# The last seven finished blocks of the first mixture are transposed by TensorE and copied by ScalarE instead of by a DMA transposition

## The chip, the cores and the metric

The kernel runs on one core of a Trainium2 chip. The metric is the device time of one execution, in microseconds (us). Engines are called by the names of the profile: PE is TensorE's matmul stream, PEld its weight loads, DVE is VectorE, ACT is ScalarE, POOL is GpSimd and SP is SyncE, which only issues DMAs here.

## What is computed

A banded attention over 3072 tokens, then two mixtures of experts in sequence. Cut to what matters here:

```python
x = attention(q, k, v, mem_k, mem_v)              # 3072 x 512
# first mixture: two experts per token
top2 = the two best of 8 noisy logits             # and their softmax weights
out[mask] += top2_w * (relu(x[mask] @ w1[e]) @ w2[e])
# second mixture: one expert per token, on the result of the first
logits = out @ w_gate2
expert_idx = argmax(logits); gate = softmax(logits)[expert_idx]
out2[mask] = gate * (relu(out[mask] @ w1b[e]) @ w2b[e])
```

The second mixture's routing needs its logits for every row that the first mixture produces, so the first mixture's last rows stand between the two.

## The kernel before

**Tiling.** Both mixtures work on blocks of 128 gathered rows. A group is two or three blocks of one expert. The first mixture has 17 groups (numbers 0 to 16, class `Moe1`); the last two, 15 and 16, are expert 7 with three blocks each, and group 16 also carries 32 remainder rows. The remainders of four experts are put together into one more block, which is finished under group number 15. For one group `mlp` does, per hidden slice f = 0 to 7, 12 matmuls into a PSUM tile `ph` (three buffers; L543), which ACT (L545) and DVE (L546) turn into the high and low fp16 halves of `hT`; then, per block, 24 matmuls of 512 columns into `py` (L554). The second mixture (`Moe2`) starts with three early groups whose rows are known before the first mixture is done, and goes on with late groups after a second routing.

**What a finished block does.** `Moe1.finish` scales `py` into `y` (ACT, L654; `y` has three buffers), scatters `y` to DRAM from POOL (L657), makes the high half of an fp16 pair `x16` (called `w` in the code; ACT, L671; two buffers) and starts a chain `rest`: DVE makes the low half (L675), a DMA on SP's queue transposes the 128 x 1024 pair into `xt` (L677), PE multiplies `xt` by the second router's weights into `lg` (`gating`, L240 and L241, eight small matmuls), DVE adds the two parts into `l` (L686) and POOL scatters `l` into the logits L in DRAM (L657).

**What sets the order.** Every engine runs its instructions in program order, and that order is written by hand: the main loop yields after each piece of a group, and a `Driver` keeps a modelled time, in which each chain sleeps for the number that it yields. The chain `rest` yields 1.2 before the low half and 8.5 after the DMA transposition. Two other chains stand in the stretch of interest: `first` (starts when groups 0 to 14 are finished) and `second` (when all are); each loads L (`lt`, L776), computes the chosen experts on DVE, counts on PE (L227 to L232), and builds a table with two `onehots` on DVE (L507 to L510) and 24 matmuls on PE (L813). From the first one's `etop` and the second one's `etab` SP reads which experts' weights to load (`stage`, L74); ACT and DVE convert these to fp16 pairs (L127, L128) between the other work. POOL gathers the second mixture's rows by the tables (`xp`, L1018), adds their halves (L1049, into an `x16` buffer), ACT and DVE make the pair `xg` (L1051, L1052), and SP's queue transposes it (L1061).

**Names for the seven blocks.** a1, a2, a3 are the blocks of group 15, b1, b2, b3 those of group 16, and r is the remainder block.

The chain that the change touches ends in these lines:

```python
t = parts("xt", 3)
nc.sync.dma_start_transpose(out=t.rearrange("p a k q -> p (a k) q"), in_=w)
yield 8.5
```

Of the kernel before, what the change touches and what calls it, by code (L numbers as in the profile page):

```python
# [6 lines left out]
F32 = mybir.dt.float32  # L7
F16 = mybir.dt.float16
I32 = mybir.dt.int32
U32 = mybir.dt.uint32  # L10
AF = mybir.ActivationFunctionType
# [171 lines left out]
def constants(tc, g, tmp):  # L183
    nc, c = tc.nc, g.c
# [7 lines left out]
    d = iota("diag", 128, F32, cm=-1, pool=tmp)  # L192
    g.ident = tmp.tile([128, 128], F32, name="ident")
    nc.vector.tensor_scalar(g.ident, d, 0.0, None, op0=OP.is_equal)
    g.ident16 = tmp.tile([128, 128], F16, name="ident16")
    nc.vector.tensor_scalar(g.ident16, d, 0.0, None, op0=OP.is_equal)
    g.tri = c.tile([128, 128], F16, name="tri")
    nc.vector.tensor_scalar(g.tri, d, 0.0, None, op0=OP.is_gt)
# [17 lines left out]
    for name, vals in (("prof", PROF), ("base", BASE[:8])):  # L216
        t = c.tile([128, E], F32, name=name)
# [19 lines left out]
def gating(nc, out, xT, w, n):  # L237

    for k in range(4):
        nc.tensor.matmul(out[:, 0:2 * n], xT[:, 0, k, :], w[:, :, k, :], start=(k == 0), stop=False)  # L240
        nc.tensor.matmul(out[:, n:2 * n], xT[:, 1, k, :], w[:, 0, k, :], start=False, stop=(k == 3))  # L241
# [321 lines left out]
class Moe1:  # L563
# [86 lines left out]
    def finish(self, p, gate, idx, group=None, lg=None):  # L650

        nc, g, tc = self.nc, self.g, self.tc
# [12 lines left out]
        def parts(name, n):  # L665
            if lg is None:
                return g.rr.tile([128, 2, 4, 128], F16, name=name, bufs=n)
            t = g.mo.tile([128, DM], F32, name="y", bufs=3).bitcast(F16)
            return t.rearrange("p (a k q) -> p a k q", a=2, k=4)
        w = parts("x16", 2).rearrange("p a k q -> p (a k q)")  # L670
        nc.scalar.activation(w[:, :DM], y, AF.Copy, scale=SX2)  # L671

        def rest(lg):
            yield 1.2
            nc.vector.scalar_tensor_tensor(w[:, DM:], y, SX2, w[:, :DM], op0=OP.mult, op1=OP.subtract)  # L675
            t = parts("xt", 3)
            nc.sync.dma_start_transpose(out=t.rearrange("p a k q -> p (a k) q"), in_=w)  # L677
            yield 8.5
            while not self.ready:
                yield 1.0  # L680
            if lg is None:
                lg = g.psr.tile([128, TB, 32], F32, name="lg")[:, 0]
            gating(nc, lg, t, g.wg2, E)
            l = g.mo.tile([128, E], F32, name="l", bufs=4)
            with nc.allow_low_precision("float32"):
                nc.vector.tensor_reduce(l, lg[:, 0:2 * E].rearrange("p (a e) -> p e a", a=2), axis=AX.X, op=OP.add)  # L686
            scatter(self.L, l)
            if group is not None:
                self.open.remove(group)
# [852 lines left out]
```

## Time and profile before

| | |
|---|---|
| median of 3 runs | 1035.58 us (1028.32 to 1047.32) |
| profiled execution, its own time | 1033.13 us |
| its span, first to last instruction | 1031.4 us |
| mean granted TensorE clock | 0.969 |
| PE busy | 951.9 us (92%) |
| DVE, ACT, POOL busy | 504.7, 386.3, 479.4 us |

The profile is of one execution. A timeline row gives start, length, engine, line, operation, and in brackets the idle time of that engine just before it with what ended it. A length of "x12" is that of twelve instructions from the first start to the last end. The granted clock is the share of full speed that TensorE was given: 1.00 is 2.4 GHz, 0.50 is 1.2 GHz.

### The profile page before, as it was taken

Reading aid. Unit: us, or ns where it says so; the run is one execution under the profiler, and the core shown is the slowest. Engines: PE = TensorE matmul, PEld = TensorE weight load, DVE = VectorE, ACT = ScalarE, POOL = GpSimd, SP = SyncE. Lnnn points to the kernel's source line nnn. Section 1 sums busy time; section 2 is a strip of 40 time slices with the busy share of each in tenths; the row PEclk is TensorE's granted clock in tenths of the full one; section 3 lists DMA queues with packets and bytes.
Section 4 is the critical chain, followed back from the end, with each engine's and each line's share of the span. In section 5 each row is a group of like instructions: output and inputs, shape, how many; then the busy total and the mean of one; then the engine's idle time right before and its main releaser. Section 6 shows DMA issues by size and latency. Waiting matters only on the chain.

```text
span 1031.4 us, 18755 instructions
## 1 busy us (share of the span) xinstructions
PE 951.9 (92%) x7259; PEld 566.5 (55%) x7259; DVE 504.7 (49%) x1032; ACT 386.3 (37%) x653; POOL 479.4 (46%) x484
## 2 busy tenths in 40 slices
PE   5897868999989999999999999985889999999998
PEld 4786745656545555455554555542457555555665
DVE  7689885642423443244332443473475436565511
ACT  2453444322323343333433343252423345454421
POOL 6755653334545454645546354335522635443421
PEclk9998969999999999999999999988899999999999
DMA  9999959745746686678766676489535879987720
GB/s 214 253 258 256 237 137 273 178 90 121 189 100 172 164 186 158 154 169 190 170 160 162 152 177 143 131 256 194 96 121 147 219 184 263 287 217 211 148 56 19
DMA packets 189218, 180.75 MB, mean 175 GB/s; under 512 B 152148, under 2 KB 153044, under 8 KB 188352
## 3 DMA queue, kind: packets, MB, share of 16 engines
q1 hardware_dynamic: 166736, 131.24, 54.2%
q0 software_dynamic: 21952, 48.07, 15.8%
q8 instruction: 60, 0.98, 0.4%
q14 instruction: 38, 0.31, 0.1%
q10 hardware_dynamic: 432, 0.15, 0.1%
HBM read 118.27 MB, written 39.53 MB: 153 GB/s over the span
## 4 chain that ended last, share of the span: by engine, by line
PE 41%; issue 16%; POOL 8%; DMA 4%; DVE 2%; ACT 0%; POOLq 0%; DVEq 0%; ACTq 0%
PE ph L543 19%; PE py L554 19%; POOL x L1049 2%; POOL xp L1018 2%; POOL out_dram L1068 2%; POOL gs L1018 2%; DMA stage<-in_v_dram 1%; PE py L736 1%; DMA xp<-Y,ter 1%; DMA xp<-Y,tbr 1%; DMA gs<-Pa,ter 1%; DMA out_dram<-y,teo 0%; DVE hT L546 0%; DMA xt<-x 0%; DVE w L128 0%
## 5 line engine op out<-in xcount | busy, mean ns | idle before, releaser
L543 PE MATMUL ph<-xT,w 128*128 128x384 f16 (+3 forms) x2688 | 426.5, 318 | 19.9 <-DVE hT L546 10.4
L554 PE MATMUL py<-w,hT 128*128 128x512 f16 x1800 | 394.2, 379 | 0.0
L543 PEld LDWEIGHTS <-w 128*128 128x128 f16 x2688 | 262.5, 99 | 166.8 <-issue 24.5
L554 PEld LDWEIGHTS <-hT 128*128 128x128 f16 x1800 | 175.7, 98 | 207.0
L546 DVE SCALAR_TENSOR_TENSOR hT<-ph,hT 128x384 f16<-128x384 f32 (+3 forms) x224 | 115.9, 521 | 218.0 <-ACT hT L545 216.9
L128 DVE SCALAR_TENSOR_TENSOR w<-stage,w 128x1024 f16<-128x1024 f32 x128 | 167.2, 1309 | 66.5 <-ACT w L127 66.3
L545 ACT ACTIVATE hT<-ph 128x384 f16<-128x384 f32 (+3 forms) x224 | 103.3, 463 | 212.6 <-PE ph L543 209.0
L127 ACT ACTIVATE w<-stage 128x1024 f16<-128x1024 f32 x128 | 133.6, 1049 | 19.1 <-DMA stage<-in_v_dram 14.3
L654 ACT ACTIVATE y<-py,gs 128x512 f32<-128x512 f32 x48 | 32.9, 686 | 176.4 <-PE py L554 170.3
L657 POOL DMA_INDIRECT L<-l,t3y x43 | 44.5, 1035 | 109.6 <-DVE l L686 106.2
L675 DVE SCALAR_TENSOR_TENSOR x<-y,x 128x512 f16<-128x512 f32 x50 | 34.4, 688 | 123.0 <-ACT x L671 122.9
L657 POOL DMA_INDIRECT Y<-y,t3y x43 | 44.8, 1041 | 91.5 <-ACT y L654 85.7
L1068 POOL DMA_INDIRECT out_dram<-y,tbo x20 | 20.8, 1039 | 110.8 <-ACT y L1067 89.0
L316 PE MATMUL s<-x 128*64 128x64 f32 x768 | 49.6, 287 | 16.3 <-DMA x<-in_xe_dram 11.6
L611 POOL DMA_INDIRECT Y<-ol,late x48 | 56.4, 1175 | 16.4 <-issue 16.4
L316 PEld LDWEIGHTS s<-x 128*64 128x64 f32 x768 | 46.3, 209 | 17.8 <-POOL x L303 8.3
L1067 ACT ACTIVATE y<-py,gs 128x512 f32<-128x512 f32 x27 | 18.6, 687 | 94.8 <-PE py L554 64.1
L370 POOL TENSOR_TENSOR x<-x,x 128x512 f16<-128x512 f32 x24 | 29.4, 1226 | 45.8 <-DVE x L369 25.1
L585 POOL DMA_INDIRECT xg<-X,t3x x43 | 42.0, 976 | 15.1 <-issue 14.6
L585 POOL DMA_INDIRECT gs<-G,t3g x41 | 38.7, 944 | 12.5 <-issue 12.5
L303 POOL COPY x<-x 24x780 f32<-24x780 f32 x48 | 41.0, 855 | 5.2 <-issue 2.5
L1049 POOL TENSOR_TENSOR x<-xp 128x512 f32<-128x512 f32 x27 | 35.9, 1355 | 15.1 <-DVE xg L1052 11.7
(276 smaller groups left out, 708.1 us busy)
## 6 DMA issues: line engine op xcount, KB each, us to landing
stage<-in_w_dram SPq DMA_DIRECT2D x64, 512.0 KB, 4.1
stage<-in_v_dram SPq DMA_DIRECT2D x64, 512.0 KB, 5.1
x<-in_xa_dram SPq DMA_DIRECT2D x24, 286.0 KB, 5.5
X<-x SPq DMA_DIRECT2D x24, 256.0 KB, 4.4
x<-in_xd_dram SPq DMA_DIRECT2D x24, 194.0 KB, 6.7
x<-in_xb_dram SPq DMA_DIRECT2D x24, 188.5 KB, 6.6
x<-in_xc_dram SPq DMA_DIRECT2D x24, 184.0 KB, 6.0
x<-in_xe_dram SPq DMA_DIRECT2D x24, 96.5 KB, 5.6
```

Source lines behind the costliest of these rows:

```text
L127: nc.scalar.activation(hi, src, AF.Copy, scale=SW)
L128: return lambda v=nc.vector: v.scalar_tensor_tensor(lo, src, SW, hi, op0=OP.mult, op1=OP.subtract)
L316: nc.tensor.matmul(s[o:o + 64, ch // 2, b], q[:, b, ch], k[:, b, 40 * ch:40 * ch + 64], start=True, stop=True)
L543: nc.tensor.matmul(p[:, :n], w1[:, a, k, f, :], xT[:, b, k, :n], start=(i == 0), stop=(i == 11))
L545: nc.scalar.activation(hT[:, 0, f, :n], p[:, :n], AF.Relu)
L546: nc.vector.scalar_tensor_tensor(hT[:, 1, f, :n], p[:, :n], 0.0, hT[:, 0, f, :n], op0=OP.max, op1=OP.subtract)
L554: nc.tensor.matmul(p[:m], hT[:, a, f, o:o + m], w2[:, c, f, :], start=(i == 0), stop=(i == 23))
L585: self.nc.gpsimd.indirect_dma_start(out=out, out_offset=None, in_=src, in_offset=IO(ap=idx, axis=0))
L611: st = nc.gpsimd.indirect_dma_start(out=self.Y, out_offset=IO(ap=idx[:, i:i + 1], axis=0), in_=z, in_offset=None, bounds_check=2 * N - 1, ...
L657: st = nc.gpsimd.indirect_dma_start(out=dst, out_offset=IO(ap=idx, axis=0), in_=src, in_offset=None, bounds_check=2 * N - 1, oob_is_err=False)
L1049: nc.gpsimd.tensor_tensor(s, x[:, :DM], x[:, DM:], op=OP.add)
L1068: st = nc.gpsimd.indirect_dma_start(out=self.out, out_offset=IO(ap=idx, axis=0), in_=y, in_offset=None, bounds_check=N - 1, oob_is_err=False)
```

## The change

For the blocks with a group number above 14 (a1 to b3 and r, seven in all), the DMA transposition is replaced by eight TensorE transposes of 128 x 128 into a `ph` tile of PSUM and one ACT copy of 128 x 1024 fp16 into `xt`. The chain's sleeps become 0.8 before and 1.0 after, instead of 8.5 after. The fp16 identity moves to the pool that lives through the whole kernel. Behind L677 all lines of the changed kernel are nine higher.

```diff
-    g.ident16 = tmp.tile([128, 128], F16, name="ident16")
+    g.ident16 = c.tile([128, 128], F16, name="ident16")
     nc.vector.tensor_scalar(g.ident16, d, 0.0, None, op0=OP.is_equal)
...
             t = parts("xt", 3)
-            nc.sync.dma_start_transpose(out=t.rearrange("p a k q -> p (a k) q"), in_=w)
-            yield 8.5
+            if group is not None and group > len(self.groups) - 3:
+
+                yield 0.8
+                o = g.pm.tile([128, 512], F32, name="ph", bufs=3).bitcast(F16).rearrange("p (i q) -> p i q", i=8)
+                for i in range(8):
+                    nc.tensor.transpose(o[:, i, :], w[:, 128 * i:128 * i + 128], g.ident16)
+                nc.scalar.activation(t.rearrange("p a k q -> p (a k) q"), o, AF.Copy)
+                yield 1.0
+            else:
+                nc.sync.dma_start_transpose(out=t.rearrange("p a k q -> p (a k) q"), in_=w)
+                yield 8.5
```

On PE, behind the first routing's count (L232) and the last block of group 15 (L554), this stood before: the 24 matmuls of a3, the hidden slice f0 of group 16, and then the gating of a1.

```order
7539 L232 MATMUL misc<-oh_8062,ones 128x8
7540 L554 LDWEIGHTS hT
7541 L554 MATMUL py<-w_2513,hT 128x512
...
7589 L554 MATMUL py<-w_2513,hT 128x512
7590 L543 LDWEIGHTS w_2512
7591 L543 MATMUL ph<-xT,w_2512 128x416
...
7614 L240 LDWEIGHTS xt
7615 L240 MATMUL lg<-wg_2518,xt 128x16
```

At the same place of the changed kernel (x_8051 is a1's pair, x_8097 a2's):

```order
7539 L232 MATMUL misc<-oh_8062,ones 128x8
7540 L682 LDWEIGHTS x_8051
7541 L682 MATMUL ph<-ident_117,x_8051 128x128
...
7556 L554 LDWEIGHTS hT
7557 L554 MATMUL py<-w_2513,hT 128x512
...
7620 L682 LDWEIGHTS x_8097
7621 L682 MATMUL ph<-ident_117,x_8097 128x128
...
7636 L543 LDWEIGHTS w_2512
7637 L543 MATMUL ph<-xT,w_2512 128x416
```

The transposes of a1 now stand ahead of a3's matmuls, the gating of a1 in the middle of them (not shown), and the transposes of a2 ahead of the whole of group 16. The transposes of a3 follow between f1 and f2.

On DVE, the low half of a2's pair (x_8097) stands in the changed kernel behind a weight conversion (L128) and the first routing's second one-hot pair, and behind it the next conversion and the low half of f0:

```order
868 L128 SCALAR_TENSOR_TENSOR w_2514<-stage,w_2514 128x1024
869 L507 TENSOR_TENSOR ol<-wide,lo_8176 128x1536
870 L509 TENSOR_TENSOR ov<-wide,col_8178 128x96
871 L510 TENSOR_TENSOR ov<-ov,tokb 128x96
872 L695 TENSOR_REDUCE l<-lg 128x8
873 L675 SCALAR_TENSOR_TENSOR x_8097<-y,x_8097 128x512
874 L128 SCALAR_TENSOR_TENSOR w_2514<-stage,w_2514 128x1024
875 L546 SCALAR_TENSOR_TENSOR hT<-ph,hT 128x416
876 L128 SCALAR_TENSOR_TENSOR w_2514<-stage,w_2514 128x1024
877 L695 TENSOR_REDUCE l<-lg 128x8
878 L675 SCALAR_TENSOR_TENSOR x_8255<-y,x_8255 128x512
```

That order is the one of before with one row put in: the sum of a1's logits (row 872) stood later.

On ACT, around the last block of group 16 and the remainder block, this stood before (`w_72` is a weight tile of the second mixture):

```order
417 L654 ACTIVATE y<-py,gs 128x512
418 L671 ACTIVATE x_8595<-y 128x512
419 L654 ACTIVATE y<-py,gs 128x512
420 L671 ACTIVATE x_8630<-y 128x512
421 L741 ACTIVATE x_8698<-py 64x512
422 L654 ACTIVATE y<-pr,gr 128x512
423 L671 ACTIVATE x_8706<-y 128x512
424 L127 ACTIVATE w_72<-stage 128x1024
425 L545 ACTIVATE hT<-ph 128x384 x2
```

And in the changed kernel:

```order
422 L683 ACTIVATE xt<-ph 128x1024
423 L654 ACTIVATE y<-py,gs 128x512
424 L671 ACTIVATE x_8679<-y 128x512
425 L683 ACTIVATE xt<-ph 128x1024
426 L750 ACTIVATE x_8756<-py 64x512
427 L654 ACTIVATE y<-pr,gr 128x512
428 L671 ACTIVATE x_8764<-y 128x512
429 L127 ACTIVATE w_72<-stage 128x1024
430 L683 ACTIVATE xt<-ph 128x1024
431 L545 ACTIVATE hT<-ph 128x384
432 L683 ACTIVATE xt<-ph 128x1024
```

The copies of b1 and b2 (the first two L683) stand around b3's `y`; the copy of b3 (the third) stands behind the remainder's three steps and a weight conversion, and the copy of r behind f0 of the second mixture's first group. On PE the gating of b3 follows b3's transposes at once (not shown).

## Rows read from the trace of the kernel before

**Rows 1.** Waits of PE, whole span: who waited for whom, total us, times, longest.
```profile
PE lg L240 <- DMA xt<-x: 15.9, 2, 11.9
```

**Rows 2.** Timeline of PE, 600 to 840 us.
```profile
660.15 5.34 PE L554 MATMUL py<-w,hT 128*128 128x512 f16 x24
...
667.64 4.38 PE L543 MATMUL ph<-xT,w 128*128 128x416 f16 x24
676.10 0.19 PE L240 MATMUL lg<-wg,xt 128*128 128x16 f16 x1 [4.07 <-DMA xt<-x]
...
676.34 4.32 PE L543 MATMUL ph<-xT,w 128*128 128x416 f16 x12
...
692.04 15.70 PE L554 MATMUL py<-w,hT 128*128 128x512 f16 x72
707.67 1.48 PE L736 MATMUL py<-w,rh 128*32 128x512 f16 x24
721.03 0.20 PE L240 MATMUL lg<-wg,xt 128*128 128x16 f16 x1 [11.88 <-DMA xt<-x]
...
746.54 7.93 PE L554 MATMUL py<-w,hT 128*128 128x512 f16 x36
...
763.31 5.40 PE L543 MATMUL ph<-xT,w 128*128 128x256 f16 x48
771.50 1.47 PE L543 MATMUL ph<-xT,w 128*128 128x256 f16 x12 [2.79 <-DVE hT L546]
...
778.07 5.34 PE L554 MATMUL py<-w,hT 128*128 128x512 f16 x24
...
791.33 10.64 PE L543 MATMUL ph<-xT,w 128*128 128x256 f16 x96
...
814.12 15.78 PE L543 MATMUL ph<-xT,w 128*128 128x384 f16 x96 [1.79 <-DMA xT<-xg]
```

**Rows 3.** Windows of PE: us, sum, busy (instructions), granted clock, DMA share, GB/s.
```profile
685.00:686.00 1.00, 1.00 (x7) 1.00 0.86 324
712.00:713.00 1.00, 0.00 (x0) 0.65 1.35 212
726.00:727.00 1.00, 1.00 (x11) 1.00 0.00 0
```

**Rows 4.** Timeline of PE in the attention: eight transposes, then the next matmul.
```profile
106.78 0.62 PE L383 MATMUL xp<-ident,x 128*128 128x128 f16 x8
107.24 0.18 PE L240 MATMUL lg<-wr,xt 128*128 128x32 f16 x1
```

**Rows 5.** Groups of ACT by form: busy us, mean ns, idle before and its releaser.
```profile
L384 ACT ACTIVATE xt<-xp 128x1024 f16<-128x1024 f16 x22 | 22.2, 1008 | 8.8 <-PE xp L383 8.8
```

**Rows 6.** Timeline of ACT, 640 to 815 us.
```profile
667.53 1.06 ACT L127 ACTIVATE w<-stage 128x1024 f16<-128x1024 f32 x1 [7.06 <-DMA stage<-in_v_dram]
...
725.64 0.59 ACT L741 ACTIVATE x<-py 64x512 f32<-64x512 f32 x1 [3.93 <-DMA xt<-x]
727.01 0.69 ACT L654 ACTIVATE y<-pr,gr 128x512 f32<-128x512 f32 x1 [0.78 <-DVE pr L742]
...
728.26 1.04 ACT L127 ACTIVATE w<-stage 128x1024 f16<-128x1024 f32 x1
```

**Rows 7.** Timeline of DVE, 640 to 815 us.
```profile
668.62 1.23 DVE L128 SCALAR_TENSOR_TENSOR w<-stage,w 128x1024 f16<-128x1024 f32 x1 [1.70 <-ACT w L127]
...
670.99 0.69 DVE L675 SCALAR_TENSOR_TENSOR x<-y,x 128x512 f16<-128x512 f32 x1
```

**Rows 8.** The tile xt, 640 to 780 us: the DMA transpositions from issue to landing.
```profile
DMA to landing us min/median/max: 3.1/4.3/19.2
```

**Rows 9.** Timeline of POOL at b1's scatter.
```profile
708.41 1.02 POOL L657 DMA_INDIRECT Y<-y,t3y  x1 [0.30 <-issue]
```

**Rows 10.** Issues of DMAs, 640 to 760 us: a scatter of y's size, us to landing.
```profile
out_dram<-y,teo POOLq DMA_INDIRECT x2, 7.1
```

**Rows 11.** Waits of PE, 810 to 1032 us.
```profile
PE ph L543 <- DVE hT L546: 3.5, 3, 1.9
```

## The prediction

> **What bounds the kernel now.** I read the waits of PE first, since PE is busy nine tenths of the span: what it waits for is what a change can give back. One wait for the operand of the second gating (`xt`, transposed by DMA) stands at the head, 15.9 us in two pieces [rows 1]. The timeline of PE places them [rows 2]: 4.07 us before 676.10, at a2, and 11.88 us before 721.03, at b1. The reader is to see that PE itself runs dry there; no other engine covers it. The tile view says why the second is long: a transposition landed 4.3 us after issue in the median and 19.2 us at worst [rows 8].
>
> The waits cost more than their length. The granted clock fell some 3 us into the second idle stretch (0.65 in 712 to 713) and came back at 685 and at 726 [rows 3], that is 8.9 and about 4.9 us after PE had work again. In between it is the 1.2 GHz level: 12 matmuls of 416 columns took 4.32 us [rows 2], where 24 took 4.38 at 2.4 GHz.
>
> So three stretches matter, by their ends in [rows 2]: A, from a3's matmuls (660.15) to the first `py` of group 16 (692.04), 31.9 us; B, from there to the first `py` of the second mixture (746.54), 54.5 us; C, the eight hidden slices of its next group (763.31 to 778.07), 14.8 us where the same 96 matmuls take 10.6 at 791.33. In C the releaser is DVE: 2.79 us for `hT`, because the second routing's table work stands in DVE's order between the slices.
>
> From 814 on PE waits 1.79 us for `xT` [rows 2] and 3.5 us for `hT` [rows 11], in 217 us. What is gained before 814 reaches the end.
>
> **The added work.** Eight transposes took 0.46 us from start to the next matmul at full clock [rows 4]; seven times that is 3.2 us of PE. One copy of 128 x 1024 took 1.008 us on ACT [rows 5]; seven are 7.1 us, on an engine with idle time but in an order that matters. Seven DMA issues leave SP's queue, so the later weight loads, the load of L and the transpositions of `xg` can only go earlier; I price that at nothing, since PE's waits after 814 are 5.3 us in all, and that is the most they could give. Moving the identity costs nothing: it is made once, at the start, as before.
>
> **Stretch A.** After the count at 660.15: transposes of a1 0.46, a3's 24 matmuls 5.2, gating 0.2, so PE is at a2's transposes at 666.0. They need a2's low half. On DVE it stands behind a weight conversion that waits for ACT's half of it, which in turn waited 7.06 us for its staged weights and began at 667.53 [rows 6]; DVE's half began at 668.62, and the low half of a2 at 670.99 with 0.69 us [rows 7]. None of this moves: the staged load follows the count, which is not later than before. With one small sum put ahead of it, the low half is ready at 671.8. Before, PE had f0 to f2 to do meanwhile (667.64 and ahead); now the transposes stand ahead of f0 and PE idles from 666.3 (four transposes need only the high half) to 671.8, 5.5 us instead of 4.07. Queued behind them is all of group 16, and the first routing's table, on which POOL's gathers wait.
>
> Then, at half clock: the other four transposes 0.4, f0 4.1 and gating 0.2, to 676.6. If the clock comes back as quickly as at 726, f1 takes 2.1 and PE waits for a3's low half (behind f0's `hT` on ACT and DVE, 0.5 and 0.6, and a conversion of 1.06 and 1.23) until about 679.9, then 0.4: 680.3. If as slowly as at 685, f1 ends at 680.8 and the transposes at 681.5. The rest, f2 to f7 (six of 2.1), gating 0.2 and 24 small table matmuls 0.7, is 13.6: `py` starts at 693.9 or 695.1. **A: 1.9 to 3.1 us longer, taken 2.5.**
>
> **Stretch B.** From the first `py`: two blocks 10.4, b1's transposes 0.5, half a block 2.6, gating 0.2 (its copy has 2.6 us of cover), half a block 2.6, b2's transposes 0.5, 24 remainder matmuls 1.4 (at 707.67 [rows 2]): 18.1. The copy for b2 stands on ACT behind b3's `y` and high half (about 1.25 together, the distance from 727.01 to 728.26 [rows 6]), so its gating waits about 0.7. Gating 0.2, the other 24 matmuls 1.4: 20.4.
>
> Here is the new wait. b3's transposes end at 20.9, but their copy stands on ACT behind the remainder's steps and a weight conversion. From the start of L741 to the end of that conversion took 3.66 us (725.64 to 728.26 and 1.04 [rows 6]); with the copy 1.0 and handovers 0.3, b3's gating starts at 25.4, a stall of 4.5. A further term: the remainder's `y` needs the buffer of b1's, whose scatter POOL started at 708.41 [rows 9]. POOL's gathers ahead of it follow the table, which is 3.4 to 4.6 later, so about 711; a scatter of that size took 7.1 to land [rows 10]. By that, up to 1.8 us more, at the other end nothing; I take 0.9, as POOL's issue after the table may be closer than before. That gives 26.3.
>
> Gating 0.2; f0 at half clock 3.9 (384 columns; full 1.97 from 15.78 for 96 [rows 2]); r's transposes 0.8; f1 2.0 or 3.9 by the two returns of the clock; gating 0.2; f2 to f7 11.8; 0.5 for the second count, which now stands ahead of `py`: 45.7 or 47.6. **B: 8.8 to 6.9 shorter, taken 7.9.** Not removed, then: of 11.88 plus half-clock work, a wait of about 5 with its own half-clock work stays.
>
> **Stretch C.** The second routing's count moves from the middle of the first group's `py` to ahead of it, so its chain on DVE runs under 15.7 us of `py`, not between the slices. Before, the count began at about 754.4 (746.54 and 7.93) and PE got on with the slices 17.1 us later, at 771.50; now `py` and the first slices, 1.3 each, cover that length. 14.8 becomes 10.6 and 0.5 that I leave for conversions: **C: 3.7 shorter.** If the count comes as late as before, nothing.
>
> **Sum.** +2.5 - 7.9 - 3.7 = -9.1. The profiled execution took 1033.13, so 1024.0. The median of the runs is 1035.58, 2.4 above it; runs lay from 1028.32 to 1047.32.
>
> **A rule against the change.** Rows: PE was granted full clock at 726 after 4.9 us of work, and in the attention, eight transposes among other matmuls took 0.46 us, 57 ns each [rows 3, 4]. The Trainium skill ("TensorE: Matmul & The Clock Gate", Part 4: PE-mode transpose) says that transposes do not count as busy for the clock and gives about 275 ns for one in a kernel. By that figure, an estimate from the page, 56 transposes one after another would be 15.4 us instead of 3.2. The rows at 106.78 do not agree, since they follow each other much closer.
>
> **The rivals.**
> - *Everything comes back* (0.10). A to C lose 4.07 and 11.88 in waits, 4.2 in C, and some 12 at half clock and in small waits behind, less 3.2 of transposes: about -29, 1004. For: the only releaser that PE names is the DMA. Against: DVE's 670.99 [rows 7] is later than the point at which PE now wants the pair.
> - *New waits take nearly all* (0.22). In B a weight conversion ahead of b3's copy waits for its staged load as one did for 7.06 us [rows 6], or the buffer of `y` comes 1.8 late, and the second count is not hidden (C gives nothing): -9.1 + 5 + 3.7 = -0.4, 1033. For: ACT and PE both work in order and ACT has waited so. Against: the load in question is issued long before.
> - *Slower: the clock stays down* (0.06). Transposes scattered behind each stall keep TensorE at 1.2 GHz through the three `py` of group 16 (15.7) and f2 to f7 of the next group (11.8); each costs its length again: -9.1 + 27.5 = +18, 1051. It decides against the change once more than 9.1 us of work that was at full clock runs at half. The page above would have it so. For: both returns took 5 us or more. Against: long matmul runs lie between the batches.
> - *The forecast* (0.62): 1024, its own range 1017 to 1031.
>
> **How the numbers follow.** The range leaves out the first rival and the slower one, 0.16, and a little of the tails; it takes in the forecast's bounds and the second rival with 2 or 3 us for the runs' own spread: 1012 to 1036. A measurement of this kernel can tell about 2% from no change, here 21 us. Faster by more needs the first rival or part of it: 0.10. Slower by more needs the clock rival at its full price and more: 0.03. Within 2%: 0.87.
>
> **What would show it.** In the changed profile PE should wait for DVE's low half ahead of f0 of group 16, about 5.5 us (A right), and for ACT's copy ahead of b3's gating, about 4.5 to 5.5 (B right), with 0.50 of the clock behind each; the wait for `xt` by DMA should be gone from these blocks. The eight slices of C should take 10.6 to 11.5 us, and everything from the first late group on should look as before, shifted. Wrong if a2's pair is ready by 667, if the gating of b3 finds its copy done, if the clock stays at 0.50 through `py`, or if a wait that is new arises after 814.

## The result, and the profile after

The changed kernel takes 1047.78 us in the median (1041.55 to 1051.8, 20 runs), the kernel before, run beside it, 1042.76 (1028.32 to 1047.32, 20 runs). The ratio is 1.0104, interval 1.0084 to 1.0124. Ratios are of executions not marked as slow: that leaves out some of the kernel before and none of the changed one here, so this ratio says 11 us where the two medians lie 5.0 apart, and the traces of before and before_again are of executions so marked. So the change costs 0.5% to 1%; forecast were 1024 and a gain of 9 us. The profiled execution of the changed kernel took 1046.33 us, with a span of 1044.6.

Lines behind L677 stand 9 further down now: L736 is L745, L741 is L750. L682 is the eight transposes of a block, L683 their copy on ACT.

The waits of PE from 640 to 840 us (who waited for whom, total us, times, longest), which answer [rows 1]:

```profile
PE ph L682 <- DVE x L675: 6.4, 3, 4.8
PE lg L240 <- ACT xt L683: 3.7, 1, 3.7
PE ph L543 <- DMA xT<-xg: 2.3, 1, 2.3
PE misc L227 <- DVE ohl L906: 2.3, 1, 2.3
PE py L745 <- issue: 1.6, 3, 1.0
PE lg L240 <- issue: 1.0, 1, 1.0
PE lg L240 <- DVE l L695: 0.6, 1, 0.6
```

The 15.9 us of waits on the DMA transposition are gone from this stretch. In their place stand a wait for DVE's low half, one for ACT's copy, one for the second count's operand, and gaps with no releaser ("issue"). The timeline of PE, which answers [rows 2], says where (start, us, line, count, idle before and its releaser):

```profile
668.93 0.25 PE L227 MATMUL misc<-oh,tri 128*128 128x192 f16 x1
...
670.16 0.61 PE L682 MATMUL ph<-ident,x 128*128 128x128 f16 x8
670.61 2.75 PE L554 MATMUL py<-w,hT 128*128 128x512 f16 x12
...
681.15 0.61 PE L682 MATMUL ph<-ident,x 128*128 128x128 f16 x4 [4.78 <-DVE x L675]
681.55 4.37 PE L543 MATMUL ph<-xT,w 128*128 128x416 f16 x12
...
703.93 10.52 PE L554 MATMUL py<-w,hT 128*128 128x512 f16 x48
...
715.50 0.40 PE L682 MATMUL ph<-ident,x 128*128 128x128 f16 x4 [0.82 <-DVE x L675]
...
721.66 1.48 PE L745 MATMUL py<-w,rh 128*32 128x512 f16 x24
...
724.43 0.42 PE L745 MATMUL py<-w,rh 128*32 128x512 f16 x3
725.15 0.38 PE L745 MATMUL py<-w,rh 128*32 128x512 f16 x1 [0.29 <-issue]
725.85 0.42 PE L745 MATMUL py<-w,rh 128*32 128x512 f16 x4 [0.33 <-issue]
727.27 1.92 PE L745 MATMUL py<-w,rh 128*32 128x512 f16 x16 [1.00 <-issue]
729.12 1.03 PE L682 MATMUL ph<-ident,x 128*128 128x128 f16 x8
733.85 0.18 PE L240 MATMUL lg<-wg,xt 128*128 128x16 f16 x1 [3.69 <-ACT xt L683]
...
754.58 0.32 PE L227 MATMUL misc<-ohl,tri 128*128 128x192 f16 x1 [2.26 <-DVE ohl L906]
...
756.80 16.25 PE L554 MATMUL py<-w,hT 128*128 128x512 f16 x72
772.88 10.64 PE L543 MATMUL ph<-xT,w 128*128 128x256 f16 x96
783.36 3.07 PE L822 MATMUL misc<-ov,ol 128*128 128x64 f16 x24
...
820.05 15.76 PE L543 MATMUL ph<-xT,w 128*128 128x384 f16 x96 [2.27 <-DMA xT<-xg]
```

At 681.15 PE has stood 4.78 us ahead of group 16's first run (a2's low half), and that run, 12 matmuls of 416 columns, takes 4.37 us, half clock (1.2 GHz); the first row is the count from which distances are taken below. At 733.85 it has stood 3.69 us for b3's copy. Ahead of that the second half of the remainder block's matmuls took 4.7 us (724.43 to 729.12), where the first half took 1.5. On ACT the copy stands where the forecast put it, behind the remainder block's steps and a weight conversion (timeline of ACT, [rows 6]):

```profile
729.23 0.59 ACT L750 ACTIVATE x<-py 64x512 f32<-64x512 f32 x1 [5.16 <-PE py L745]
730.59 0.69 ACT L654 ACTIVATE y<-pr,gr 128x512 f32<-128x512 f32 x1 [0.78 <-DVE pr L751]
731.31 0.63 ACT L671 ACTIVATE x<-y 128x512 f16<-128x512 f32 x1
731.85 1.04 ACT L127 ACTIVATE w<-stage 128x1024 f16<-128x1024 f32 x1
732.79 1.00 ACT L683 ACTIVATE xt<-ph 128x1024 f16<-128x1024 f16 x1
```

The granted clock shows that each of these waits is paid twice, by its own length and by slower matmuls behind it (windows: us, sum, PE busy (instructions), clock, DMA share, GB/s; [rows 3]):

```profile
668.93:682.93 14.00, 9.22 (x79) 0.87 0.62 208
696.93:710.93 14.00, 14.00 (x74) 1.00 0.96 303
724.93:738.93 14.00, 8.76 (x63) 0.76 0.07 25
```

In the first and the last window, with the two long waits, PE has 9 busy us of 14 and the clock is at its lower level (1.2 GHz) for a quarter and for half of the time; between them PE is busy throughout at 1.00.

There is a loss that the stretch doesn't hold. About 55 us behind the start of the late groups (814.12 in before [rows 2], 820.05 after) ACT waits for a weight chunk, and PE behind it for `hT`. First before's row of ACT, then the changed kernel's row of ACT and its rows of PE:

```profile
867.80 1.06 ACT L127 ACTIVATE w<-stage 128x1024 f16<-128x1024 f32 x1 [3.91 <-DMA stage<-in_v_dram]
```

```profile
878.36 1.06 ACT L127 ACTIVATE w<-stage 128x1024 f16<-128x1024 f32 x1 [8.54 <-DMA stage<-in_v_dram]
```

```profile
874.68 6.01 PE L543 MATMUL ph<-xT,w 128*128 128x384 f16 x36 [1.40 <-DMA xT<-xg]
885.66 9.62 PE L543 MATMUL ph<-xT,w 128*128 128x384 f16 x42 [4.97 <-DVE hT L546]
```

The conversion of the chunk starts 53.7 us behind the late groups' start in the one, 58.3 in the other. The wait for `xT` at 874.68 is new too: it is 0.6 to 2.6 us long in four traces of the changed kernel, and no trace of a kernel that turns by DMA alone has it (timelines of PE).

So I split each trace in three: the **head** to the first routing's count, the **stretch** from there to the first late group's run, and the **late part** from there to the last matmul. "Fifth run" is the late run that waits for the chunk. In us, worked out from the timelines of PE; the kernels with other names are told of below; each is one of the two kernels unchanged, or before with the identity's place alone. The count of before's trace, from which its stretch starts:

```profile
658.92 0.25 PE L227 MATMUL misc<-oh,tri 128*128 128x192 f16 x1
```

| kernel | head | stretch | late part | fifth run | waits on `xt` by DMA in the stretch |
|---|---|---|---|---|---|
| before | 658.9 | 155.2 | 212.2 | 17.7 | 15.9 |
| ident_only | 671.5 | 142.5 | 212.5 | 18.0 | 7.0 |
| before_look | 667.9 | 150.8 | 216.2 | 20.3 | 8.7 |
| after | 668.9 | 151.1 | 219.4 | 23.4 | none |
| after_again | 666.4 | 151.3 | 217.3 | 21.9 | none |
| after_look | 673.1 | 154.9 | 218.4 | 21.2 | none |
| after_third | 669.0 | 156.0 | 218.6 | 23.4 | none |

Means of the three and of the four: head 666.1 and 669.4, stretch 149.5 and 153.3, late part 213.6 and 218.4. The differences of the last two are 3.8 and 4.8 us, 8.6 of the 11 that the ratio says; the head spreads over 13 us in the first three alone and holds little of the change (the identity's place and a1's first steps). How the loss divides is not shown by so few traces: the stretch, for which the forecast was made, spreads over 13 us in the same three, and against ident_only alone it would carry 10.8 us and the late part 5.9. What repeats is the late part, 217.3 to 219.4 in the four traces of the changed kernel and 212.2 to 216.2 in the three others.

### The profile page after: what moved, and what is told of

Same layout as the page of the kernel before. It is cut to its first block, busy times and chain, and to the rows that moved or that the text cites. A ratio compares the mean times of both kernels' runs of the same rounds, so it can differ in the third digit from the quotient of the medians.

```text
span 1044.6 us, 18855 instructions
## 1 busy us (share of the span) xinstructions
PE 964.5 (92%) x7315; PEld 574.3 (55%) x7315; DVE 499.6 (48%) x1032; ACT 391.0 (37%) x660; POOL 477.7 (46%) x484
## 4 chain that ended last, share of the span: by engine, by line
PE 39%; issue 16%; POOL 8%; DMA 4%; DVE 2%; ACT 1%; POOLq 0%; DVEq 0%; ACTq 0%
PE ph L543 19%; PE py L554 18%; POOL gs L1027 2%; POOL xp L1027 2%; DMA stage<-in_v_dram 2%; POOL out_dram L1077 2%; POOL x L1058 2%; DMA xp<-Y,ter 1%; PE py L745 1%; DVE w L128 1%; DMA xp<-Y,tbr 1%; DMA xt<-x 1%; DVE hT L546 1%; PE misc L822 0%; POOL Y L657 0%
## 5 line engine op out<-in xcount | busy, mean ns | idle before, releaser
L554 PE MATMUL py<-w,hT 128*128 128x512 f16 x1800 | 395.1, 379 | 0.0
L554 PEld LDWEIGHTS <-hT 128*128 128x128 f16 x1800 | 175.7, 98 | 207.2 <-issue 0.8
L128 DVE SCALAR_TENSOR_TENSOR w<-stage,w 128x1024 f16<-128x1024 f32 x128 | 164.5, 1288 | 70.1 <-ACT w L127 68.3
L127 ACT ACTIVATE w<-stage 128x1024 f16<-128x1024 f32 x128 | 133.7, 1049 | 24.9 <-DMA stage<-in_v_dram 20.5
L657 POOL DMA_INDIRECT L<-l,t3y x43 | 44.6, 1037 | 111.9 <-DVE l L695 107.7
L611 POOL DMA_INDIRECT Y<-ol,late x48 | 54.4, 1133 | 16.4 <-issue 16.4
```

The source lines that it names most:

```text
L127: nc.scalar.activation(hi, src, AF.Copy, scale=SW)
L128: return lambda v=nc.vector: v.scalar_tensor_tensor(lo, src, SW, hi, op0=OP.mult, op1=OP.subtract)
L554: nc.tensor.matmul(p[:m], hT[:, a, f, o:o + m], w2[:, c, f, :], start=(i == 0), stop=(i == 23))
L611: st = nc.gpsimd.indirect_dma_start(out=self.Y, out_offset=IO(ap=idx[:, i:i + 1], axis=0), in_=z, in_offset=None, bounds_check=2 * N - 1, ...
L657: st = nc.gpsimd.indirect_dma_start(out=dst, out_offset=IO(ap=idx, axis=0), in_=src, in_offset=None, bounds_check=2 * N - 1, oob_is_err=False)
```

## The experiments

The kernel before ran beside each of the others on the same chip, and ratios are to that. Chips differ: its median was 1026.57 us beside both_late, before_pad and after_pad, and 1037 to 1042 beside the rest. Kernels are told apart by ratio; what their traces say is one execution each.

### The two kernels again, and the identity's place

before_again is the kernel before, after_again the changed one. ident_only is before with one line of the change:

```
-    g.ident16 = tmp.tile([128, 128], F16, name="ident16")
+    g.ident16 = c.tile([128, 128], F16, name="ident16")
```

later is the changed kernel with longer pauses, so that the transposes and the gatings stand further back in PE's order:

```
-                yield 0.8
+                yield 5.0
...
-                yield 1.0
+                yield 3.5
```

> The kernel before, unchanged, for a second trace of it. Split the span at the first routing's count (L227 on oh: 658.9 us in the first trace) and at the first late group's matmuls (814.1): head 658.9, stretch 155.2, tail 217.3. If the first trace was a quick draw in its head and tail (theory 1), this one has a head of 662 to 670, the same stretch of 153 to 157, and a ratio of 1.000. If instead the stretch varies (theory 3: the DMA transpositions mostly land sooner than in the first trace), the stretch is 145 to 150 and the waits for xt are under 8 us in all.

> The changed kernel, unchanged, for a second trace. First trace: head 668.9, stretch 151.1, tail 224.6. If the head and tail vary by execution, they move by several us here (theory 1); if the change causes them, they stay within 2 us (theory 2, by the move of the identity in the memory; theory 4, by the order). Ratio 1.008 to 1.012 in any case.

> The kernel before with only the identity in the lasting pool, so that all tiles after it lie 256 bytes higher per partition; the DMA transpositions stay. Theory 2 (the shift of addresses costs in the head): ratio 1.005 to 1.010 and a head of 666 to 671. Theories 1, 3 and 4: ratio 1.000 within 0.002.

> The changed kernel with the chain's two sleeps longer (5.0 and 3.5 instead of 0.8 and 1.0), so that a2's transposes stand behind f1 of group 16, and b3's behind the remainder. If the cost sits in PE waiting ahead of f0 for the low half (4.8 us, and half clock), this kernel is 4 to 8 us quicker than the changed one, ratio 1.002 to 1.006 to before. If the cost lies in head and tail, it stays at 1.008 to 1.012.

Measured: before_again 1.0013 (0.9974 to 1.0051), after_again 1.0115 (1.0071 to 1.0159), ident_only 1.0011 (0.9976 to 1.0046), later 1.0037 (1.0006 to 1.0068). The loss repeats. The identity's place does nothing that the ratio can tell, so theory 2 falls. before_again's trace (head 674.4, stretch 150.2, late part 216.1, waits on `xt` 11.3) fits neither of the cases that I gave and is not in the means above. after_again's head and late part came 2.5 and 2.2 us below the first trace's, between its two cases. ident_only's trace and that of before_look (below) have the same gating of b1 as [rows 2] at 721.03, in the same order (timelines of PE, before_look and ident_only):

```profile
720.61 0.20 PE L240 MATMUL lg<-wg,xt 128*128 128x16 f16 x1 [4.27 <-DMA xt<-x]
```

```profile
722.40 0.18 PE L240 MATMUL lg<-wg,xt 128*128 128x16 f16 x1 [2.72 <-DMA xt<-x]
```

The 11.88 us of the first trace are 4.27 and 2.72 here (6.42 in before_again, 4.50 in before_pad, below); a2's wait, 4.07 there, stays at 4.40 and 4.32. That is theory 3: the execution that I took the term from had an unusually long wait in this place. later got 7 of the 11 us back by order alone: group 16's first run starts 6.9 us behind the count, as in before (6.4), not 12.6. Its stretch is 145.6 us, its late part 217.8.

### Which part costs, and what there is to win

a_only has TensorE turn a1 to a3 alone, b_only the remainder block and b1 to b3 alone, a_later is a_only with later's pauses. no_turn is before in its own order with the last seven not turned.

```
 a_only:  if group == len(self.groups) - 2 and p is not self.pr:
 b_only:  if group is not None and (group == len(self.groups) - 1
                  or group > len(self.groups) - 3 and p is self.pr):
 no_turn: if group is not None and group > len(self.groups) - 3:
              t = w.rearrange("p (a k q) -> p a k q", a=2, k=4)
```

> The kernel before, in its own order, but the last seven blocks are not turned at all: their gating matmuls read the rows as they lie, so the logits of these blocks are other numbers and the choice that hangs on them too. It shows the most that any way of turning could gain. Theory 1 (the waits on the DMA transpositions are a real cost, 7 to 16 us by the execution): no xt wait is left between the count and the late groups, the stretch from the count to the late groups falls to 138-143 us, the ratio is 0.986-0.993. Rival (other waits stand right behind them): the stretch stays at 145 us or more and the ratio is 0.995-1.000.

> Only group 15's three blocks (a1 to a3) are turned by TensorE, the other four by DMA. If the price of the changed kernel lies in the wait ahead of group 16's first f run: that run begins 12-13.5 us behind the count (6.4 in before), one wait on a DMA transposition of group 16 stays (3-12 us), ratio 1.004-1.012. If it lies in the four later blocks: ratio 0.998-1.003. If the late stall around 870 us comes with the a part, the tail is 222-225 us, else 217-218.

> Only the remainder block and group 16's three blocks are turned by TensorE, group 15's by DMA as before. If the price lies ahead of group 16's f run: that run begins 6-7 us behind the count, the stretch is 143-147 us, ratio 0.994-1.000. If it lies in the copies and waits of the four later blocks: stretch 150 or more, ratio 1.004-1.010. If the late stall around 870 us comes with this part, the tail is 222-225 us, else 217-218.

> Group 15's three blocks by TensorE with both pauses lengthened as in the run called later, the other four by DMA. If what the longer pauses gave lies in the a part alone: group 16's f run at 6.5-7 us, its py run at 28-30, ratio 0.996-1.001; against later (1.0037) it tells what the four later blocks cost. If the four later blocks bring nothing and cost nothing: ratio 1.002-1.005, as later.

Measured: a_only 1.0026 (0.9991 to 1.006), b_only 1.0004 (0.9975 to 1.0034), a_later 1.004 (1.0008 to 1.0072). no_turn's whole time, 1.0883 (1.0828 to 1.0938), says nothing, since other choices give the late groups other loads; its stretch does, since the same matmuls run in it. Stretch and late part: a_only 151.9 and 215.1, b_only 148.3 and 215.0, a_later 150.6 and 216.7; no_turn's stretch is 144.0. That lies between the two cases that I gave (138 to 143, 145 or more), as b_only's does (143 to 147, 150 or more), and no_turn's ratio is far from 0.986 to 0.993.

The two parts together cost 11 us, each alone 0 to 3. I had expected one of them to be guilty; neither is, and what the two do to each other stays open. In a_only group 16's first run starts 13.2 us behind the count, as in the changed kernel, yet the ratio is 1.0026: by that, the wait at a2 alone is not the price of 11 us. In a_later the places came as expected (group 16's first run at 6.9 us, its `py` at 28.7), but not the ratio of 0.996 to 1.001. b1's transposition, by DMA there, was late again (timeline of PE), which I took for the reason; a_later_b13 below speaks against it:

```profile
723.79 0.20 PE L240 MATMUL lg<-wg,xt 128*128 128x16 f16 x1 [8.39 <-DMA xt<-x]
```

no_turn's one trace is the nearest to a bound on the gain. With nothing to turn, a gating still waits 5.12 us, for DVE's read of the logits ahead of it (timeline of PE), and the stretch is 144.0:

```profile
742.78 0.17 PE L240 MATMUL lg<-wg,x 128*128 128x16 f16 x1 [5.12 <-DVE l L689]
```

Against the first trace's 155.2 that is 11 us to win; against the mean of 149.5, under 6; against ident_only's 142.5, nothing.

### The pause in place of the engine

longer is before with all seven blocks turned by DMA, and more work between transposition and gating. a_later_b13 is a_later with the same pause for the four blocks that it leaves to DMA. after_look and before_look are the two kernels once more, for a trace.

```
-            yield 8.5
+            yield 13.0 if group is not None and group > len(self.groups) - 3 else 8.5
```

> The kernel before, all seven blocks still turned by DMA, but the pause between the transposition and the gating is 13.0 in place of 8.5, so that TensorE has one or two more runs ahead of each gating. If what costs is that the gating stands too early for a transposition that lands late: the waits on xt between the count and the late groups fall from 7-16 us to under 3, the stretch to 142-147 us, ratio 0.991-0.998. Rival (the choice and the tables then start later and TensorE waits for them, or hT and l waits take their place): stretch 148 or more, ratio 0.999-1.004.

> As a_later (group 15's three blocks by TensorE with long pauses), and the remainder block and group 16's by DMA with the pause 13.0. If the 8.4 us that a_later waited on a DMA transposition are cover that a later gating finds: the wait falls under 3 us, the stretch from 150.6 to 143-146, ratio 0.994-1.000. If not: stretch about 150, ratio 1.002-1.006.

> The changed kernel once more, for one more trace of it. If the long wait for a weight chunk some 50 us behind the start of the late groups belongs to the change: the fifth run of the late part takes 21.5-23.5 us again and the part from the late groups to the last matmul 217 us or more. If it is chance: 17.5-20 us and 212-215. The stretch is 150-152 in either case, if its waits are the fixed ones that two traces showed.

> The kernel before once more. If the long wait for a weight chunk belongs to the change: the fifth run of the late part takes 17-18.5 us and the part from the late groups to the last matmul 212-213. If it is chance: anything from 17 to 23 us. The stretch lies anywhere in 142-156 us, with 7 to 16 us of waits on DMA transpositions.

Measured: longer **0.9957** (0.9922 to 0.9992), a_later_b13 1.0048 (1.0013 to 1.0083). longer is quicker than both kernels, than before by about 0.5%. Its waits of PE from 640 to 840 us have no line for `xt`; the longest line is many short waits:

```profile
PE ph L543 <- DVE hT L546: 7.1, 6, 2.0
```

Its stretch is 141.5 us, no longer than no_turn's: the landing time could be covered, and there were runs of PE to cover it with. That the waits on `xt` are what longer gained is not shown by the traces, though: ident_only's stretch is 142.5 us with 7.0 us of these waits in it, before_pad's (below) 141.8 with 7.6. a_later_b13's expectation failed. Its wait for DMA went, its stretch fell to 147.7, and its ratio did not move; its trace has 9.5 us of `hT` waits in 6, and a late part of 216.4.

That pair on one chip says more. Neither kernel waits for a DMA transposition into `xt` in the stretch, in both group 16's first run starts 6.4 to 6.9 us behind the count, and a_later_b13 waits 1.0 us for a copy on ACT and not at all ahead of its transposes. What is left between them is that TensorE turns a1 to a3, in another order; and a_later_b13 is 9.7 us slower in the median, with intervals that do not meet. So covered waits alone do not make the turning by TensorE free, and where those 9.7 us come from stays open: the stretches differ by 6.2 us, the late parts by 5.5.

after_look's trace showed the changed kernel's waits once more, 6.9 us for DVE ahead of the transposes, 7.2 for the copy, 2.2 ahead of the second count; its stretch of 154.9 is outside the 150 to 152 that I gave. Its fifth run of 21.2 lies just under the bound that I gave for a cost of the change, and its late part (218.4) within it; before_look's 20.3 and 216.2 are more than that theory allowed the kernel before. The two theories' cases met in the middle, so these two traces alone settle nothing.

### Does turning by TensorE cost anything, and why is the late part longer

both_late is the changed kernel with pauses of 5.0 and 8.0, in sum longer's 13.0. before_pad and after_pad put small matmuls at the program's start, where PE waits for its first input: 56 (before_pad: as many more instructions as the changed kernel has) and 72 (after_pad: 256 more than before in all).

```
             constants(tc, g, ld)
+            pad = at.ps.tile([128, 512], F32, name="s", bufs=2)
+            for _ in range(56):
+                nc.tensor.matmul(pad[:, 0:8], g.ones, g.ones[:, 0:8], start=True, stop=True)
```

> All seven blocks by TensorE as in the changed kernel, but with pauses of 5.0 ahead of the transposition and 8.0 behind it, in sum the 13.0 that the run called longer has around its DMA transposition; no wait is meant to be left on either way of turning, so against longer (0.9957) it gives the price of turning by TensorE itself. Theory 1 (the changed kernel lost by where its steps stand and by the late part): no wait of over 1 us on the copies or ahead of the transpositions, stretch 141.5 + 3 to 5 us for 56 transpositions and 7 copies, 144-147; ratio 0.999-1.002 if the late part stays at 216-219 us. Rival (the turning by TensorE was no cost, only its places): stretch 141-143, late part 211-213, ratio 0.994-0.997.

> The kernel before with 56 small matmuls into a scratch tile at the program's start, while TensorE waits for its first input: as many more instructions ahead of everything else as the changed kernel has by its transpositions. If the late part's longer wait for a weight chunk hangs on where TensorE's instructions lie in the program (its instruction fetches move against the rest): the fifth late run takes 20.5-23 us, the late part 216-219, ratio 1.002-1.006. If not: as before, 16-21 us and 211-216, ratio 0.998-1.002.

> The changed kernel with 72 small matmuls at the program's start, so that with its transpositions it has 256 instructions more than before, which the trace's instruction fetches of 16 KB make one whole fetch. If the late part's longer wait hangs on the place of the fetches: the fifth late run falls to 16-20 us, the late part to 211-215, ratio 1.003-1.007 in place of 1.011. If not: 21-23 us, 217-219, ratio 1.009-1.013.

Measured: both_late 1.0014 (0.9979 to 1.0048), before_pad 1.0025 (0.9991 to 1.006), after_pad 1.0032 (1.0 to 1.0064).

In both_late the waits of PE from 640 to 840 us on either half of the new work are 1.5 us in sum:

```profile
PE ph L543 <- DVE hT L546: 11.4, 7, 2.8
PE ph L543 <- DMA xT<-xg: 2.3, 1, 2.3
PE ph L682 <- DVE x L675: 0.9, 2, 0.5
PE ph L682 <- ACT xt L683: 0.6, 1, 0.6
```

and the clock stays up through the two places at which the changed kernel lost it (windows, the same distances behind the count):

```profile
655.81:669.81 14.00, 12.26 (x94) 1.00 0.66 223
711.81:725.81 14.00, 14.00 (x111) 1.00 0.72 104
```

Its stretch is 142.9 us, between longer's 141.5 and longer2's 144.6 (below), with 56 transposes and 7 copies in it. So in this one trace's stretch turning by TensorE cost nothing measurable once little waited for it. By the ratios both_late is about 0.6% behind longer all the same; the two ran on different chips and their intervals overlap, so that is likely, not shown. Its trace has a late part of 217.2 us and a fifth run of 21.6, against longer's 210.9 and 16.4 (215.0 and 20.5 in longer2). The ratio is the first theory's, the stretch the rival's; a price, if there is one, stands in another place than I put it.

before_pad's fifth run is 21.6 and its late part 216.1, as the theory of the instruction fetches wanted, but before_look has 20.3 and 216.2 with no padding, and before_pad's ratio is not clear of 1. after_pad's ratio is as the theory wanted, its fifth run of 20.8 lies between the two cases, and its late part of 217.6 is against it. after_pad's ratio is below the changed kernel's, but from another chip, so both ran once more, beside each other, with longer a second time:

> The changed kernel, on the same chip as the next two. If the padding at the program's start gave the changed kernel something (after_pad came to 1.0032 on another chip than the one on which the changed kernel came to 1.0115): ratio 1.008-1.013 here. If it was the chip: 1.002-1.005. In the trace: 5 us ahead of group 16's first f run, 3.5-4.2 us ahead of the gating behind the remainder block's second half, 2.2 us ahead of the second count, each time; what varies is what lies between the halves of the remainder block's matmuls (0.3 to 4.6 us).

> The changed kernel with the 72 small matmuls at the start, beside after_third. If the place of the instruction fetches costs the changed kernel: 1.002-1.006, 4 us or more below after_third, and under 1 us between the halves of the remainder block's matmuls. If not: within 2 us of after_third.

> The kernel before with the pause 13.0 ahead of the last seven gatings, a second time on another chip. If what the first run showed (0.9957) holds: 0.992-0.999, no wait over 1 us on a DMA transposition between the count and the late groups, the stretch 140-143 us. If it was chance: 0.998-1.003.

Measured: after_third 1.0117 (1.007 to 1.0164), after_pad2 1.0051 (1.0014 to 1.0088), longer2 0.9951 (0.9911 to 0.9991). longer's gain repeats; its stretch of 144.6 is outside the 140 to 143 that I gave. The padded kernel is the quicker one beside the changed kernel too, by 7 us in the medians, with intervals that overlap a little, and 72 matmuls of no use, some 670 us ahead, are all that sets it apart. after_third's waits stand where I expected them (7.3 us for DVE ahead of the transposes, 7.7 for the copies, 2.3 ahead of the second count). One place where the padding shows is the remainder block's second half. In the changed kernel (after_look's timeline of PE) the gating between the halves waits and the second half runs at half clock; in after_pad the one is short and the other runs at full clock:

```profile
730.63 0.18 PE L240 MATMUL lg<-wg,xt 128*128 128x16 f16 x1 [3.11 <-ACT xt L683]
730.91 3.49 PE L745 MATMUL py<-w,rh 128*32 128x512 f16 x24
```

```profile
711.56 0.18 PE L240 MATMUL lg<-wg,xt 128*128 128x16 f16 x1 [0.50 <-ACT xt L683]
711.85 1.48 PE L745 MATMUL py<-w,rh 128*32 128x512 f16 x24
```

But after_pad2 has it otherwise again: 1.0 us and gaps at this place, a stretch of 152.7, and its gain in the late part (213.0, fifth run 18.1). That these instructions help the changed kernel is made likely by two runs; that it is by the place of those behind them, or in which way, is not shown.

The late part stays open too. Its fifth run is 16.4 to 21.6 us in six traces of kernels that turn by DMA alone (the three above, longer 16.4, longer2 20.5, before_pad 21.6), 21.2 to 23.4 in the four of the changed kernel, 18.1 to 21.6 in eight others with TensorE (among them later 21.6, a_only 20.6, b_only 20.5, after_pad2 18.1). So it goes with the turning by TensorE, but loosely. In before and after, ACT's weight conversions and SP's issues of weight loads and transpositions in the last 20 us ahead of the wait stand at the same distance from the late groups' start, to 0.4 us; what differs is what the DMA engines moved. In the 24 us from 36 us behind that start (GB/s in 40 slices of 0.6 us), before and after:

```profile
GB/s 0 0 0 116 232 375 242 121 32 166 259 232 437 266 280 44 146 169 125 80 189 143 177 408 376 437 430 355 417 437 437 329 330 369 396 437 437 423 369 410
```

```profile
GB/s 0 0 0 102 259 416 168 163 244 197 266 365 229 102 21 75 103 121 102 120 86 80 86 83 73 127 100 72 314 438 314 410 417 437 382 382 424 336 349 430
```

The slow piece in the middle, with gathers and transpositions under way, is 8 slices long before (44 to 189) and 15 after (21 to 127). The load that ACT waits for lands behind it. Why the piece is longer is not shown.

## Why the prediction was wrong, step by step

**What bounds: the waits on the transposition. Right in place, wrong in size.** The step that failed first is that a wait of one execution was taken for the kernel's: 11.88 us at b1 [rows 2], from a landing of 19.2 where the median was 4.3 [rows 8]. The spread stood in the row that I quoted, and I read it for the wrong transposition: the 19.2 is that of the one issued behind b1's, at 706.38, and b1's, issued at 703.57 (timeline of SP), let PE go on at 721.03, 17.5 us later. The stretch is 142.5 to 155.2 us in three traces with before's order (ident_only among them), and the sum was made against the longest. The same trace has the shortest head, 658.9 against 667.9 and 671.5, so that its whole time, 1033, looked typical and hid that. Trace against trace, the 1046.33 us measured lie 22.3 above the 1024.0 forecast: 10.0 in the head, where the trace that the sum started from was a short one, 5.0 in the stretch (151.1, where 155.2 less 9.1 was forecast) and 7.2 in the late part, which was to stay as it was.

**Stretch A, right.** From the end of the count to group 16's first `py`: 670.16 to 703.93, 33.8 us, 1.9 more than the 31.9 of before; forecast 1.9 to 3.1. (Against before_look's 30.1 and ident_only's 29.8 it is about 4 more.) The wait of 5.5 was 4.78: a2's low half started at 680.41 on DVE, which is 670.4 less the head's 10.0, where [rows 7] had it at 670.99:

```profile
680.41 0.68 DVE L675 SCALAR_TENSOR_TENSOR x<-y,x 128x512 f16<-128x512 f32 x1
```

f0 at half clock took 4.16 to the next instruction (4.1 in the forecast).

**Stretch B, the mis-sized term.** Forecast 45.7 to 47.6 us; 703.93 to 756.80 is 52.9. Against the 54.5 of the trace that the sum was made with, that is 1.6 shorter, not 7.9; against the same stretch in before_look (48.3) and ident_only (43.2) it is longer. By its pieces: up to the end of the first remainder half 18.1 was forecast and 19.2 measured, as b1's transposes found no low half (0.82), which I had not looked up. From there to the end of the second half 2.3 forecast, 6.0 measured: the wait of 0.7 was 1.0, the matmuls' 1.4 were 4.7, with gaps. From there to b3's gating 5.9 forecast, 4.7 measured: the named wait was right, and `y`'s buffer did not come late. Around the second count 0.5 was forecast and 4.5 measured, 2.26 of wait and 2.2 for the count. So the order was read right, and the large wait in it; the small steps, 0.82 + 6.0 + 4.5 = 11.3 us where 2.8 stood, were not. Part of that is the clock: the eight transposes at 729.12 take 1.03 us, those at 670.16 0.61 by the same measure.

**Stretch C, right.** The eight slices take 772.88 to 783.36, 10.5 us, forecast 10.6 to 11.5. From the second mixture's first `py` to the late groups the changed kernel needs 63.2, before 67.6 (68.2 in ident_only, 71.1 in before_look): 4.3 gained or more, forecast 3.7.

**"What is gained before 814 reaches the end." Wrong.** By the means the late part grew by 4.8 us. The forecast named the condition ("a wait that is new arises after 814"), but gave it no price: 5.3 us of PE waits were read as the most that could be given, not as a place where more could be lost. The transpositions of `xg`, which by the forecast could "only go earlier", are waited for ahead of the fifth run (1.40), where before has no wait.

**The rivals.** "New waits take nearly all" (0.22, 1033) was nearest in mechanism: ACT and PE in order, a small handover at each. Its price missed the same two things, the typical wait of before and the late part. "The clock stays down" (0.06, 1051) was nearest in number, by luck, for it did not happen: behind the wait at 681 the clock is back at 1.00 for 696 to 710. The transposes were as cheap as [rows 4] had them: 0.45 us for eight (670.16 to 670.61), 1.03 at half clock by the length of their row (729.12). The Trainium skill ("TensorE: Matmul & The Clock Gate", Part 4: PE-mode transpose) has about 275 ns for one; no run here agrees: by its own row one lasts 219 ns in the median of the 56, and eight of them overlap, 0.45 us or 56 ns each. Whether transposes count as work for the clock, the page's other half, no run here tests.

**Range and chances.** 1012 to 1036 did not reach 1047.78. Its upper end was the second rival and 3 us; the medians of before alone, 1035.58 of the first three runs and 1042.76 of twenty, moved by more than that. The change is within 2%, as 0.87 had it, on the other side of 1.

## What to carry to other kernels

A wait in one trace is one draw. If a DMA's landing spreads from 3 to 19 us [rows 8], take its wait from several executions before pricing what removes it; here the same wait was 2.72 to 11.88. To get rid of a wait on a transfer, first ask whether other work can stand between the transfer and its use: one number (8.5 to 13.0) gave 0.5%, where moving the work to two engines that run in order put waits for DVE, for ACT and ahead of the second count where one kind had been, and cost 0.5% to 1%. And where such work is moved to PE and ACT all the same, it should stand where its operand is done and its result is not yet wanted: later and both_late got most of the loss back that way. It need not be enough, as a_later_b13 shows.

## What the runs showed of the hardware

- The two waits of PE of 4.78 and 3.69 us in the changed kernel had the granted clock at 0.87 and 0.76 over the 14 us around them; both_late, which doesn't wait there, had 1.00 at the same distances. 12 matmuls of 416 columns took 4.37 us behind such a wait, 24 took 4.38 at 699.71 in the same trace.
- The same DMA transposition, in the same order of issue, made PE wait 11.88, 4.27 and 2.72 us in three executions (before, before_look, ident_only).
- 72 matmuls of no use at the start of the program went with a changed kernel 7 us quicker in the median (1.0117 and 1.0051 on one chip, with intervals that overlap a little). Where it comes from is open: one trace has it in the stretch, another in the late part.
- The DMA engines' slow piece in the late part, at 134 GB/s in the mean before and 90 after, lasted 5 us before and 9 after, with the issues ahead of it at the same distances to 0.4 us.
- A transpose of 128 x 128 on TensorE lasts 219 ns by its own row, in the median of 56; eight behind one another took 0.45 us to the next matmul at full clock.
